# A new written order, other first loads and one slot array in a chunk attention and phase mixing kernel

## The chip, the cores and the metric

The kernel runs on one core of one Trainium2 chip. The metric is the time of one execution on the device in microseconds (us). One execution was also taken by the hardware profiler; all rows come from that trace. Engines: PE is TensorE (PEld its weight loads), DVE is VectorE, ACT is ScalarE, POOL is GpSimd, SP is SyncE, which only issues transfers here. The loads that POOL issues here change the type on the way (fp32 to fp16); the transfers of SP and ACT change no type.

## What is computed

There are 8 batches of 8 heads, 576 positions and 64 columns. First comes attention inside chunks of 64 positions, then a mixing layer over the 512 = 8 x 64 columns:

```
scores = q_c @ k_c^T / 8;  attn = softmax(scores);  x = attn @ v_c
theta = x @ w_theta
y = w_tok_r @ (x * cos(theta)) + w_tok_i @ (x * sin(theta))      # over positions
u = x + y
out = u + max(u @ w_ch, 0)
```

## The kernel before, in words

Batches go in four pairs, numbered 0 to 3. The 1152 positions of a pair are nine tiles of 128 rows: 0 to 3 of the first batch, 4 to 7 of the second, and 8 (MID), which holds the last 64 positions of both. Attention works on groups: A (tiles 0, 1), B (2, 3), C (4, 5), D (6, 7), M (8).

All work is written by hand as a list of steps, `ORDER`; each step calls one function, and each engine and each queue runs its own part of the list strictly in that order. A step is kind.place.slot: `S.0A.0` is the scores of pair 0, group A, into PSUM bank 0; `Y.12.7` is the mixing of pair 1, tile 2, in bank 7. For copies the last number is a buffer slot. The kinds:

- `qk` (load_qk, L161, issued at L168 and L173) and `v` (load_v, L180, issued at L192): loads by POOL, cast to fp16 on the way. `lt`, `ct` (L202, L205): w_theta in fp32 by SP, and its cast, half on ACT (L208), half on DVE (L210). `lc` (L212): w_ch by POOL. `lw` (L197): 128 rows of the token weights by POOL, in two transfers (L200).
- `Tq`, `Tk`, `T` (L248): DVE's 32 x 32 transposes of q and k (L257). `S` (L264): scores on PE (L272). `E` (L282): exp on ACT (L286). `V0`, `V1` (L293): products with v for heads 0 to 3 and 4 to 7 on PE (L306); v has a column of ones, so that they also give the row sums. `N0`, `N1` (L315): DVE's reciprocal (L321) and product (L323).
- `X` (L332): transposes of x on PE (L338), then `xa` or `xv`, a copy from PSUM on ACT (L358) or DVE (L356); or, in the place of both, `xd`, a transposing transfer by SP (L350).
- `H` (L364): x @ w_theta on PE (L370). `G` (L379): cos and sin on ACT (L384, L388); exp and sin lie in different tables, and a table load stands in front of an activation that needs the other one. `Z` (L392): zr = x cos, zi = x sin on DVE (L398 to L405).
- `TW`, `twv`, `twa` (L217, L232): PE's transposes of the token weights (L227) and their copies (L237 on DVE, L239 on ACT).
- `Y` (L431): nine matmuls of 512 columns a tile (L420); `Ya` and `Yb` are its first four and last five. `A` (L439): u = x + y on DVE (L441). `U` with `ua` or `uv` (L443, L449), or `ud` by SP (L454): the transpose of u. `W` (L462): u @ w_ch on PE (L466). `R` (L471): relu and sum on DVE (L473). `st`, `sa` (L479): the store on SP's or ACT's queue (L484, L487).
- `pre` (L136): fills of zeros, the column of ones, a first exp. `init` (L152): the identity, by POOL. `dm.n` (L155): n matmuls of zeros (L157).

Buffers come from a pool with one tag for each name and slot: eight for q and k, others for T, eT, xT, cos, sin, uT and o. The order begins and ends so:

```
pre.00 lt.00 ct.00 qk.0A.0 Tq.0A.0 Tk.0A dm.16.7 S.0A.0 v.0A E.0A.0 dm.4.7 V1.0A.2
init.00 V0.0A.4 ct.01 N0.0A N1.0A dm.8.7 X.0A.6 xa.0A.0 qk.0M.1 Tq.0M.1 Tk.0M dm.4.7
H.0A.0 S.0M.7 qk.0B.2 Tq.0B.2 E.0M.1 v.0M dm.11.7 V0.0M.4 Tk.0B v.0B lw.01 V1.0M.5
S.0B.2 N1.0M N0.0M dm.2.7 X.0M.6 E.0B.2 V1.0B.4 xa.0M.1 N1.0B V0.0B.2 N0.0B H.0M.7
G.0A.0 TW.01.4 twv.01 lw.03 X.0B.6 TW.03.2 lw.02 dm.1.5 TW.02.4 xv.0B.2 Z.0A twv.03
G.0M.1 Z.0M twa.02 H.0B.0 lw.00 Ya.02.6 G.0B.2 Z.0B qk.0C.3 Tq.0C.0 Tk.0C Ya.01.7
...
W.30.4 sa.27 R.36.2 sa.31 R.34.1 ud.38.0 ud.37.3 st.26 W.38.5 W.37.6 R.30.0 R.38.3 sa.30
st.36 R.37.5 sa.37 st.34 st.38
```

Of the kernel before, what the change touches and what calls it, by code (L numbers as in the profile page):

```python
# [38 lines left out]
Z.1D E.2A.1 V0.2M.7 R.10.3 V0.2A.3 V1.2A.0 V1.2M.5 N1.2A xa.2B.2 N0.2A W.07.2 Y.15.6
U.13.0 ua.13.1 N0.2M X.2A.1 qk.2C.5 xv.2A.3 R.07.2 H.2B.3 G.2B.1 N1.2M Z.2B T.2C.0  # L40
W.13.7 X.2M.0 xa.2M.0 H.2A.1 qk.2D.6 R.13.4 T.2D.2 v.3C H.2M.5 v.2D W.11.3 R.11.1 st.06
G.2A.2 qk.3A.7 Y.14.0 st.10 G.2M.0 sa.11 Z.2A A.15 ud.15.5 S.2D.1 S.2C.3 Z.2M Y.16.7
A.16 ud.16.6 E.2D.2 V1.2D.5 V0.2D.1 A.14 ud.14.4 N1.2D N0.2D E.2C.0 st.05 v.2C Y.18.3
V1.2C.4 N1.2C V0.2C.6 W.12.0 qk.3D.0 Y.21.1 A.18 qk.3B.1 A.21 N0.2C Y.23.4 Y.22.5
xd.2D.1 sa.07 st.13 T.3A.1 R.12.0 Y.17.6 xd.2C.2 H.2C.2 A.17 T.3B.2 H.2D.6 qk.3C.2 A.22
T.3C.0 A.23 Y.20.0 G.2C.1 v.3B S.3C.1 S.3A.3 U.18.5 A.20 Z.2C v.3A G.2D.2 W.14.6 st.12
Z.2D qk.3M.3 W.16.7 U.17.0 T.3D.0 v.3M R.16.3 ua.18.0 Y.24.5 E.3C.1 A.24 W.18.1 R.18.5
R.14.1 Y.26.2 T.3M.1 ud.20.2 S.3B.5 ua.17.1 S.3M.7 S.3D.0 st.16 A.26 E.3A.3 V0.3A.3
N0.3A E.3B.2 V1.3A.5 E.3M.0 W.15.2 N1.3A R.15.2 Y.25.7 ud.21.0 A.25 V1.3B.3 V0.3B.5
E.3D.3 V0.3M.0 v.3D N0.3M V1.3M.1 sa.14 W.17.2 N0.3B xd.3A.3 sa.18 N1.3B Y.27.7 W.21.0  # L50
# [14 lines left out]
def kernel(  # L65
# [23 lines left out]
    VP = D + 2  # L89
    scale = 1.0 / math.sqrt(D)  # L90
    half = [slice(0, CH), slice(CH, P)]
    quarter = [slice(32 * i, 32 * i + 32) for i in range(4)]

# [14 lines left out]
    bufs = ctx.enter_context(tc.tile_pool(name="bufs", bufs=1))  # L108
# [10 lines left out]
    wnat = const.tile([P, KT + 1, 2, S], FP16, name="wnat")  # L119
    v16 = const.tile([P, 2 * NT, H, VP], FP16, name="v16")  # L120
    wraw = const.tile([P, NDB, DM], FP32, name="wraw")
# [5 lines left out]
    def buffer(shape, name, slot, dtype=FP16):  # L127
        return bufs.tile(shape, dtype, name=name, tag=f"{name}{slot}")
# [6 lines left out]

    def setup(p, g):  # L136
        nc.vector.memset(zeros, 0.0)
        nc.vector.memset(pihalf, math.pi / 2.0)  # L138

        one = tmp.tile([P, 2, 32, 2], FP16, name="one")  # L140
# [6 lines left out]
        nc.vector.tensor_copy(  # L147
            out=v16[:, :, :, D], in_=one[:, 1, 0:H, 0].unsqueeze(1).broadcast_to((P, 2 * NT, H))
        )
        nc.scalar.activation(out=first, in_=pihalf, func=AF.Exp)  # L150
# [10 lines left out]
    def load_qk(p, g, slot):  # L161
        j0, bb, s0 = GROUPS[g]
        t = buffer([P, 2, H, 2, D], "qk", slot)
        st["qk", p, g] = t
        for w, ap in enumerate((q, k)):
# [6 lines left out]
            else:  # L172
# [5 lines left out]
                )  # L178

# [17 lines left out]
    def load_tok(p, tb):  # L197
        rows = min(P, S - tb * P)
        for ri, ap in enumerate((moe_w_tok_r, moe_w_tok_i)):
            nc.gpsimd.dma_start(wnat[0:rows, tb, ri], ap[tb * P : tb * P + rows, :])  # L200

    def load_theta(p, g):  # L202
        nc.sync.dma_start(wraw, moe_w_theta.rearrange("(a p) e -> p a e", p=P))

    def cast_theta(p, a):  # L205
        h = slice(2 * a, 2 * a + 2)
        if a == 0:
            nc.scalar.copy(out=wtheta16[:, h], in_=wraw[:, h])  # L208
        else:
            nc.vector.tensor_copy(out=wtheta16[:, h], in_=wraw[:, h])  # L210
# [6 lines left out]
    def tok_w(p, tb, b):  # L217
        m = min(P, S - tb * P)
        rows = slice(0, m)
        ps = banks(b, 2, FP16)[:, 0 : NT * m].rearrange("p (k t) -> p k t", k=NT)  # L220
        for kt in range(NT):
# [4 lines left out]
            for to, ri, s0, n in parts:  # L226
                nc.tensor.transpose(  # L227
                    ps[to, kt, :], wnat[rows, tb, ri, s0 : s0 + n], id16[rows, rows]
                )
# [311 lines left out]
```

## Time and profile before

| what | value |
|---|---|
| three runs | 202.27, 202.6 (median), 204.76 us |
| span of the profiled execution | 202.3 us |
| mean granted clock of TensorE | 0.986 |
| busy: PE, DVE, ACT, POOL | 183.1, 134.0, 90.5, 85.8 us |
| read from and written to HBM | 33.06 MB, 9.44 MB |
| POOL's queue: bytes written to the chip | 16.01 MB |

The profile gives no time of the whole execution beside the span, from the first to the last instruction; it lies 0.3 us under the median of the runs. A row of the timeline has its start, its length, the engine and line, the operation with out<-in, its count and, in brackets, how long the engine had stood idle and what ended that. A row of groups has busy time, mean ns of one, and idle time before. A row of windows has for each engine the busy time and, in brackets, the count of instructions, then the granted clock, the share of the transfer engines and GB/s. "Issue" is idle time for which the profile shows no release. Matmuls overlap in the records, so that busy PE time is not work.

### The profile page before, as it was taken

Reading aid. Unit: us, or ns where it says so; the run is one execution under the profiler, and the core shown is the slowest. Engines: PE = TensorE matmul, PEld = TensorE weight load, DVE = VectorE, ACT = ScalarE, POOL = GpSimd, SP = SyncE. Lnnn points to the kernel's source line nnn. Section 1 sums busy time; section 2 is a strip of 40 time slices with the busy share of each in tenths; the row PEclk is TensorE's granted clock in tenths of the full one; section 3 lists DMA queues with packets and bytes.
Section 4 is the critical chain, followed back from the end, with each engine's and each line's share of the span. In section 5 each row is a group of like instructions: output and inputs, shape, how many; then the busy total and the mean of one; then the engine's idle time right before and its main releaser. Section 6 shows DMA issues by size and latency. Waiting matters only on the chain.

```text
span 202.3 us, 5964 instructions
## 1 busy us (share of the span) xinstructions
PE 183.1 (90%) x2600; PEld 91.6 (45%) x2600; DVE 134.0 (66%) x240; ACT 90.5 (45%) x97; POOL 85.8 (42%) x121
## 2 busy tenths in 40 slices
PE   7369899999999998699899999799999999999980
PEld 2134554564546534354554444354644444444320
DVE  3137078888569777576867976657787965563560
ACT  2222199557993477059749700098404370400000
POOL 7587994795985867279564730000000000000000
PEclk9979999999999999999999999999999999999997
DMA  5999999999999999999999999605197865442776
GB/s 196 170 106 172 166 166 173 158 172 165 116 168 164 177 155 211 174 195 167 197 232 177 212 132 123 196 0 81 32 203 159 164 126 155 131 141 77 240 203 200
DMA packets 104602, 32.13 MB, mean 159 GB/s; under 512 B 97792, under 2 KB 99456, under 8 KB 104576
## 3 DMA queue, kind: packets, MB, share of 16 engines
q0 software_dynamic: 77232, 16.01, 99.9%
q1 hardware_dynamic: 24576, 10.75, 26.3%
q10 hardware_dynamic: 2768, 4.98, 7.1%
q8 instruction: 20, 0.33, 0.7%
q14 instruction: 6, 0.05, 0.2%
HBM read 33.06 MB, written 9.44 MB: 210 GB/s over the span
## 4 chain that ended last, share of the span: by engine, by line
PE 67%; DMA 12%; ACT 6%; DVE 5%; issue 4%; SPq 3%; POOL 0%; ACTq 0%; DVEq 0%; POOLq 0%
PE psum L420 25%; PE psum L466 13%; PE psum L370 13%; DMA uT<-x 5%; PE psum L272 5%; DMA qk<-in_k_dram 4%; PE psum L157 3%; PE psum L306 3%; DMA xT<-x 2%; PE psum L338 2%; SPq L350 2%; ACT eT L286 2%; ACT sin L388 2%; DVE T L257 2%; PE psum L227 1%
## 5 line engine op out<-in xcount | busy, mean ns | idle before, releaser
L192 POOL DMA_DIRECT2D v<-in_v_dram x56 | 41.7, 763 | 16.1 <-DMA qk<-in_k_dram 6.8
L420 PEld LDWEIGHTS <-wT 128*128 128x128 f16 (+1 forms) x360 | 30.8, 100 | 37.1 <-issue 3.0
L420 PE MATMUL psum<-zr,wT 128*128 128x512 f16 (+1 forms) x180 | 44.5, 381 | 0.0
L420 PE MATMUL psum<-zi,wT 128*128 128x512 f16 (+1 forms) x180 | 42.0, 379 | 1.6 <-issue 1.6
L441 DVE TENSOR_TENSOR x<-psum,x 128x512 f16<-128x512 f32 x36 | 24.5, 682 | 19.4 <-PE psum L420 18.1
L466 PE MATMUL psum<-wch,uT 128*128 128x512 f16 x144 | 35.4, 380 | 0.6 <-DMA uT<-x 0.3
L370 PE MATMUL psum<-wtheta,xT 128*128 128x512 f16 x144 | 33.8, 380 | 1.6 <-DMA xT<-x 1.0
L257 DVE STREAM_TRANSPOSE T<-qk 128x1024 f32<-128x1024 f32 (+3 forms) x25 | 25.0, 1013 | 7.6 <-DMA qk<-in_q_dram 6.8
L473 DVE SCALAR_TENSOR_TENSOR o<-psum,x 128x512 f32<-128x512 f32 x36 | 24.1, 681 | 6.8 <-PE psum L466 6.3
L384 ACT ACTIVATE cos<-psum,pihalf 128x1024 f16<-128x1024 f32 (+1 forms) x20 | 20.6, 1031 | 13.8 <-PE psum L370 13.4
L286 ACT ACTIVATE eT<-psum 128x1024 f16<-128x1024 f32 (+1 forms) x20 | 18.4, 939 | 18.6 <-PE psum L272 18.0
L323 DVE TENSOR_TENSOR x<-psum,recip 128x512 f16<-128x512 f32 (+1 forms) x40 | 25.5, 638 | 1.4
L384 ACT ACT_TABLE_LOAD x8 | 10.3, 1283 | 26.1 <-PE psum L370 20.1
L370 PEld LDWEIGHTS <-xT 128*128 128x128 f16 x144 | 13.3, 98 | 18.5 <-ACT xT L358 2.1
L466 PEld LDWEIGHTS <-uT 128*128 128x128 f16 x144 | 13.0, 98 | 15.5 <-DMA uT<-x 1.9
L272 PE MATMUL psum<-T 32*64 32x64 f16 x1152 | 13.9, 193 | 5.9 <-DVE T L257 5.0
L388 ACT ACTIVATE sin<-psum 128x1024 f16<-128x1024 f32 (+1 forms) x20 | 18.7, 937 | 0.0
L321 DVE RECIPROCAL recip<-psum 128x8 f32<-128x8 f32 (+1 forms) x40 | 7.8, 194 | 14.5 <-PE psum L306 14.1
L398 DVE TENSOR_TENSOR zr<-x,cos 128x1024 f16<-128x1024 f16 x16 | 11.0, 685 | 9.5 <-ACT cos L384 9.5
L173 POOL DMA_DIRECT2D qk<-in_q_dram x16 | 14.7, 917 | 5.4 <-DVE zi L399 2.3
L272 PEld LDWEIGHTS <-T 32*64 32x64 f16 x1152 | 11.9, 106 | 10.1 <-DVE T L257 6.0
L157 PE MATMUL psum<-zeros 128*128 128x512 f16 x46 | 14.6, 470 | 1.9 <-DVE pihalf L138 1.2
(43 smaller groups left out, 130.5 us busy)
## 6 DMA issues: line engine op xcount, KB each, us to landing
out_dram<-o ACTq DMA_DIRECT2D x17, 256.0 KB, 2.9
qk<-in_q_dram POOLq DMA_DIRECT2D x16, 256.0 KB, 7.5
qk<-in_k_dram POOLq DMA_DIRECT2D x16, 256.0 KB, 8.4
out_dram<-o SPq DMA_DIRECT2D x15, 256.0 KB, 3.9
v<-in_v_dram POOLq DMA_DIRECT2D x40, 64.0 KB, 7.3
v<-in_v_dram POOLq DMA_DIRECT2D x16, 128.0 KB, 8.2
wraw<-in_moe_w_theta_dram SPq DMA_DIRECT2D x1, 1024.0 KB, 5.5
wnat<-in_moe_w_tok_r_dram POOLq DMA_DIRECT2D x4, 144.0 KB, 5.0
```

Source lines behind the costliest of these rows:

```text
L192: nc.gpsimd.dma_start(v16[rows, slot + t, :, 0:D], v[b, :, t0 : t0 + m, :].rearrange("h s d -> s h d"),)
L257: nc.vector.transpose(to.bitcast(FP32).rearrange("p (x l s) -> p x s l", l=32, s=2), src.bitcast(FP32).rearrange("p (x s d) -> p x s d", s ...
L272: nc.tensor.matmul(ps[half[r ^ cc], r, h], t[quarter[c], 1, h, :, e], t[quarter[c], 0, h, :, e], start=(e == 0), stop=(e == 1), tile_posit ...
L286: nc.scalar.activation(out=eT[:, 0:n].rearrange("p r h i -> p (r h i)"), in_=st.pop(("ps_s", p, g)).rearrange("p r h i -> p (r h i)"), fun ...
L323: nc.vector.tensor_tensor(out=x.rearrange("p r (h d) -> p r h d", h=H // 2), in0=ps[:, :, :, 0:D], in1=recip[:, 0:n].broadcast_to((P, n, H ...
L370: nc.tensor.matmul(ps[:, j * DM : j * DM + DM], xT[:, j, a, :], wtheta16[:, a, :], start=(a == 0), stop=(a == NDB - 1),)
L384: nc.scalar.activation(out=cos[:, 0:n].rearrange("p j e -> p (j e)"), in_=ps, func=AF.Sin, bias=pihalf, scale=1.0,)
L388: nc.scalar.activation(out=sin[:, 0:n].rearrange("p j e -> p (j e)"), in_=ps, func=AF.Sin)
L420: nc.tensor.matmul(ps[half[b]] if j == MID else ps, w, z, start=(kt == 0), stop=(kt == 2 * KT),)
L441: nc.vector.tensor_tensor(out=x, in0=st.pop(("ps_y", p, j)), in1=x, op=ALU.add)
L466: nc.tensor.matmul(ps, uT[:, a, :], wch16[:, a, :], start=(a == 0), stop=(a == NDB - 1))
L473: nc.vector.scalar_tensor_tensor(out=o, in0=st.pop(("ps_w", p, j)), scalar=0.0, in1=st["x", p][:, j], op0=ALU.max, op1=ALU.add,)
```

## The change

- *First loads.* Group A of pair 0 comes by SP in fp32, in two halves of four heads (`qk0`, `qk1`: four transfers of 256 KB), and is cast in halves: `cx0` (q on DVE, k on ACT), `cv1` (both on DVE). Its T, S, E are made in halves too (`T0`, `S0`, `E0` and `T1`, `S1`, `E1`). POOL makes the identity and then loads groups M and B and the v of all three.
- *w_theta* comes by POOL, cast on the way (`lp`), behind those v.
- *Zeros* for the dummies are filled behind DVE's first cast; the column of ones (`on`) behind T1. There are 27 dummies instead of 46.
- *Tables.* Ahead of each E and G that needs the other table stands a one-element activation of that kind, which carries the table load and waits for no TensorE result.
- *One slot array.* q, k, T, token weights and the cos and sin of two-tile groups share 2048-column slots; eT, xT, o and the one-tile cos and sin share 1024-column slots; uT has 512-column slots. A step takes the slot that its last number names, and waits for the last reader of what was there.
- *Phase step by tile.* For 0A and 0B, `H0`, `G0`, `Z0` and `H1`, `G1`, `Z1` work on one tile each. `Ya` and `Yb` have four matmuls each, and `Ym` the ninth.
- *The last tile* in halves of 256 columns: `W0`, `R0`, `st0` and `W1`, `R1`, `sa1`. Four stores go by POOL (`sg`).
- *A new order.* U is made by TensorE for six tiles instead of nine.

The diff, cut to its core:

```diff
+NSLOTS = {"big": 19, "mid": 14, "uT": 10}
 ORDER = """
+init.00 qk0.0A.0 cx0.0A.1 qk1.0A.2 pre.00 dm.2.0 dm.4.1 qk.0M.3 dm.2.0 dm.12.1 Tq.0M.4 Tk.0M
+T0.0A.0 qk.0B.5 Tq.0B.3 Tk.0B S0.0A.2 S.0B.0 E0.0A.0 cv1.0A T1.0A E.0B.1 S.0M.2 v.0A v.0B dm.2.3
+v.0M S1.0A.4 on.00 V0.0A.6 lp.00 dm.1.0 N0.0A lw.01.1 V0.0B.0 N0.0B V1.0B.6 dm.4.3 E.0M.2
+V1.0M.0 N1.0B lw.00.0 E1.0A V1.0A.1 X.0B.3 lw.02.4 N1.0A N1.0M X.0A.6 xa.0B.3 H1.0B.1 G1.0B.0
+xv.0A.1 H1.0A.6 TW.01.2 G1.0A.4 H0.0A.0 V0.0M.1 N0.0M lw.03.2 H0.0B.7 twv.01 G0.0A.1 X.0M.6
+Z1.0A xa.0M.3 Z0.0A G0.0B.2 Z0.0B TW.00.4 twv.00 TW.02.2 twv.02 TW.03.0 twa.03 Ya.01.7 Z1.0B
+H.0M.6 G.0M.2 Ya.00.2 Ya.02.3 Yb.02 qk.0C.3 Tq.0C.2 Z.0M Ym.02 v.0C Tk.0C Yb.00 Ym.00 A.00
...
+N0.0C Yb.03 Ym.03 S.0D.0 A.01 U.01.7 N1.0C X.0C.4 qk.1A.4 T.1A.1 v.0D xv.0C.0 ua.01.1 v.1A
+S.1A.2 A.03 E.0D.2 V0.0D.4 N0.0D V1.0D.0 qk.1M.3 N1.0D H.0C.6 X.0D.4 lw.04.4 xv.0D.2 E.1A.3
+G.0C.1 V1.1A.0 V0.1A.2 H.0D.4 TW.04.6 N1.1A G.0D.2 Z.0C Ya.05.0 twa.04 N0.1A Ya.04.2 X.1A.3
+Ya.06.4 Z.0D Yb.06 Ym.06 qk.1B.0 T.1B.4 A.06 Yb.04 U.03.6 Yb.05 T.1M.0 Ym.05 A.05 Ym.04 ua.03.2
+U.02.6 S.1B.4 E.1B.2 v.1B A.04 qk.2B.1 Y.08.0 lc.00 xv.1A.3 ua.02.3 V1.1B.6 V0.1B.4 T.2B.4
+S.2B.2 N1.1B W.03.1 S.1M.6 E.1M.0 v.1M N0.1B X.1B.4 A.08 W.00.5 E.2B.2 U.04.6 uv.04.2 V0.1M.0
...
+E.2D.6 ud.17.3 R.13.8 qk.3M.4 X.2A.4 T.3M.3 S.3A.5 E.3A.10 Y.18.1 A.18 V0.2C.5 X.2M.2 N0.2C
+ud.15.0 W.07.3 v.2D R.07.1 xa.2A.11 H.2A.0 st.13 xv.2M.8 R.10.12 V0.2D.2 N0.2D V1.2D.4 Y.16.7
+G.2A.4 qk.3B.5 N1.2D H.2M.0 G.2M.6 xd.2C.13 xd.2D.11 T.3B.2 H.2C.1 A.16 ud.11.2 W.15.0 Z.2M
+H.2D.6 ud.12.5 st.04 G.2C.5 W.11.1 Z.2B V1.3A.2 Z.2A ud.14.0 qk.3D.0 Y.22.4 Z.2C ud.18.4 G.2D.6
...
+R.27.5 ud.35.5 sg.26 sg.22 W.38.3 Y.34.1 A.34 A.31 R.38.1 sa.03 Y.32.7 W.30.0 ud.31.4 Y.37.3
+R.30.10 A.37 W.36.0 A.32 R.36.4 st.30 ud.34.3 ud.37.7 W.21.1 R.21.10 W.31.7 ud.32.0 sa.38 sa.36
+sa.21 R.31.1 W.20.0 R.20.3 W.33.1 W.34.7 sg.27 st.31 st.20 R.33.5 sa.33 W.35.0 R.34.4 sa.34
+R.35.10 st.35 W.32.1 R.32.1 W0.37.7 R0.37.5 st0.37 W1.37.0 R1.37 sa.32 sg.25 sa1.37
 """.split()
...
+    arrays = {
+        name: const.tile([P, NSLOTS[name] * w], FP16, name=name)
+        for name, w in (("big", 2048), ("mid", 1024), ("uT", 512))
+    }
...
+    def table(func):
+        if st.get("table") != func:
+            nc.scalar.activation(out=first, in_=pihalf, func=func)
+            st["table"] = func
...
+    def load_qk_half(f):
+        def load(p, g, slot):
+            j0, bb, s0 = GROUPS[g]
+            t = big(slot, 1, FP32).rearrange("p (w h s d) -> p w h s d", w=2, h=HH, s=2)
+            st["stage", f] = t
+            for w, ap in enumerate((q, k)):
+                nc.sync.dma_start(
+                    t[:, w].rearrange("p h s d -> p h (s d)"),
+                    ap[2 * p + bb, f * HH : f * HH + HH, s0 : s0 + GT, :].rearrange(
+                        "h (p s) d -> p h (s d)", s=2
+                    ),
+                )
...
+    def cast_qk_half(f, engines):
...
+            for w, e in enumerate(engines):
+                copy = nc.scalar.copy if e == "a" else nc.vector.tensor_copy
+                copy(out=to[:, w], in_=t[:, w])
...
+    def load_theta_cast(p, g):
+        nc.gpsimd.dma_start(wtheta16, moe_w_theta.rearrange("(a p) e -> p a e", p=P))
...
+    def theta_tile(j):
+        def step(p, g, b):
+            ps = banks(b)
+            theta_mms(ps, st["xT", p, g][:, j])
+            st["ps_t", p, g, j] = ps
...
     KTS = {
-        "": range(2 * KT + 1),
-        "a": [0, 1, KT, KT + 1],
-        "b": [2, 3, KT + 2, KT + 3, 2 * KT],
+        "a": [0, KT, 1, KT + 1],
+        "b": [2, KT + 2, 3, KT + 3],
+        "m": [2 * KT],
     }
+    KTS[""] = KTS["a"] + KTS["b"] + KTS["m"]
...
+    def w_half(f):
+        def step(p, j, b):
+            ps = banks(b)[:, 0 : DM // 2]
+            channel_mms(ps, st["uT", p, j], columns[f])
+            st["ps_w", p, j, f] = ps
```

More of the change, by code (lines that the diff above doesn't have):

```diff
@@ L89 @@
     VP = D + 2
+    HH = H // 2
     scale = 1.0 / math.sqrt(D)
@@ L291, in exps, with exps_half, step @@
         )
+    def exps_half(f):
+        def step(p, g, slot=None):
+            if f == 0:
+                st["eT", p, g] = mid(slot).rearrange("p (r h i) -> p r h i", r=2, h=H)
+            table(AF.Exp)
+            nc.scalar.activation(
+                out=st["eT", p, g][:, :, f * HH : f * HH + HH],
+                in_=st.pop(("ps_s", p, g, f)),
+                func=AF.Exp,
+                scale=scale,
+            )
+        return step
     def attn(f):
@@ L360, in x_copy, with theta_mms @@
         return copy
+    def theta_mms(ps, xT):
+        for a in range(NDB):
+            nc.tensor.matmul(
+                ps, xT[:, a, :], wtheta16[:, a, :], start=(a == 0), stop=(a == NDB - 1)
+            )
     def theta(p, g, b):
```

289 lines of the change are left out of this document (172 added, 117 removed).

## The prediction

> **What bounds the kernel now.** I read the page first, then the chain of waits, the windows, and the timeline of the start, the stalls and the end.
>
> ```profile
> span 202.3 us, 5964 instructions
> ...
> PE 183.1 (90%) x2600; PEld 91.6 (45%) x2600; DVE 134.0 (66%) x240; ACT 90.5 (45%) x97; POOL 85.8 (42%) x121
> ...
> PE 67%; DMA 12%; ACT 6%; DVE 5%; issue 4%; SPq 3%; POOL 0%; ACTq 0%; DVEq 0%; POOLq 0%
> ```
>
> TensorE carries the chain. But busy time counts overlapping records and 46 dummies, so I price its real work from undisturbed pieces of the chain (start, us, what):
>
> ```profile
> 28.19 0.62 PE psum L227 x10
> ...
> 37.19 0.64 PE psum L272 x64
> ...
> 46.33 0.45 PE psum L306 x32
> ...
> 51.41 0.45 PE psum L338 x8
> ...
> 172.70 3.88 PE psum L420 x18
> ```
>
> A 512-column matmul takes 3.88/18 = 0.2156 us, a token transpose step TW 0.6, a score group S 0.64, both halves of V 0.45, a transpose 0.056. With 36 Y tiles of nine (69.8), 288 matmuls of H and W (62.1), 20 S (12.8), V (8.8), 92 X and 36 U transposes (5.2, 2.0) and TW (3.0), the real work is 163.7 us. The other 202.3 - 163.7 = 38.6 us are lost. Where?
>
> ```profile
> 10.00:20.00 10.00, 8.09 (x127) 3.84 (x128) 5.85 (x11) 2.04 (x2) 8.00 (x13) 0.83 1.62 138
> ...
> 190.00:203.00 13.00, 6.53 (x28) 2.30 (x26) 4.54 (x7) 0.00 (x0) 0.00 (x0) 0.89 0.71 217
> ```
> ```profile
> 1.19 5.75 PE L157 MATMUL psum<-zeros 128*128 128x512 f16 x16 [1.19 <-DVE pihalf L138]
> ...
> 6.28 1.04 ACT L208 CAST wtheta<-wraw 128x1024 f16<-128x1024 f32 x1 [4.05 <-DMA wraw<-in_moe_w_theta_dram]
> ...
> 9.39 0.71 DVE L257 STREAM_TRANSPOSE T<-qk 128x512 f32<-128x512 f32 x1 [6.85 <-DMA qk<-in_q_dram]
> 9.65 0.58 POOL L168 DMA_DIRECT2D qk<-in_k_dram  x1 [2.01 <-DMA qk<-in_q_dram]
> 10.90 0.71 DVE L257 STREAM_TRANSPOSE T<-qk 128x512 f32<-128x512 f32 x1 [0.80 <-DMA qk<-in_k_dram]
> ...
> 11.54 1.02 DVE L210 CAST wtheta<-wraw 128x1024 f16<-128x1024 f32 x1
> 11.67 0.71 PE L272 MATMUL psum<-T 32*64 32x64 f16 x64 [4.73 <-DVE T L257]
> ...
> 21.80 0.56 POOL L200 DMA_DIRECT2D wnat<-in_moe_w_tok_i_dram  x1
> ...
> 32.63 0.59 PE L420 MATMUL psum<-zr,wT 128*128 128x512 f16 x2
> ```
>
> Until the first Y at 32.6 TensorE has done S and V of three groups (1.9 + 1.3), X (1.1), 20 matmuls of H (4.3) and three TW (1.9), 10.5 us: 22.1 are lost there. At the end 28 matmuls (6.0 us) fill 190.0 to 196.9, 0.9 lost, and 5.4 follow: 6.3. The middle loses 38.6 - 22.1 - 6.3 = 10.2. Its visible waits:
>
> ```profile
> 75.66 0.70 PE L272 MATMUL psum<-T 32*64 32x64 f16 x64 [0.50 <-ACT sin L388]
> 76.73 0.69 PE L272 MATMUL psum<-T 32*64 32x64 f16 x62 [0.36 <-ACT sin L388]
> ...
> 82.91 1.04 PE L420 MATMUL psum<-zi,wT 128*128 128x512 f16 x4 [1.64 <-issue]
> ...
> 129.25 3.63 PE L370 MATMUL psum<-wtheta,xT 128*128 128x512 f16 x16 [1.01 <-DMA xT<-x]
> ```
> ```profile
> 0.00:82.50 82.50, 72.39 (x1247) 37.63 (x1247) 53.91 (x101) 46.07 (x49) 61.66 (x89) 0.98 1.70 165
> 0.00:99.70 99.70, 88.61 (x1503) 46.40 (x1503) 65.67 (x122) 57.25 (x61) 73.68 (x104) 0.98 1.75 167
> 0.00:116.50 116.50, 104.46 (x1759) 54.66 (x1759) 79.44 (x147) 68.09 (x73) 84.16 (x119) 0.99 1.76 173
> ...
> q8 instruction: 20, 0.33, 0.7%
> ...
> PE psum L306 <- issue: 1.9, 3, 0.9
> ```
>
> The windows end at three stalls put down to "issue" (with a fourth 1.64 + 1.9 = 3.5 us). Matmuls done by then: 1247, 1503, 1759, steps of 256, each with a weight load; and 0.33 MB in 20 fetches is 16 KB a fetch, about 5200/20 = 256 TensorE instructions. So I read these as waits for the next block of instructions, after blocks of small S and V matmuls.
>
> **The change, part by part.** *Start.* First q, k come as four 256 KB fp32 loads on SP. What SP moved in the first 15 us (40 slices of 0.375 us):
>
> ```profile
> GB/s 0 0 0 0 0 158 82 289 333 388 388 415 393 310 190 181 171 154 172 182 177 167 155 147 155 153 167 174 173 116 125 29 10 11 52 61 72 159 182 180
> ```
> ```profile
> L257 DVE STREAM_TRANSPOSE T<-qk 128x512 f32<-128x512 f32 x8 | 5.3, 686 | 7.6 <-DMA qk<-in_q_dram 6.8 <-DMA qk<-in_k_dram 0.8
> L323 DVE TENSOR_TENSOR x<-psum,recip 128x512 f16<-128x512 f32 x32 | 22.1, 692 | 1.1
> L384 ACT ACT_TABLE_LOAD x8 | 10.3, 1283 | 26.1 <-PE psum L370 20.1 <-DVE x L323 4.8 <-issue 1.1
> L384 ACT ACTIVATE cos<-psum,pihalf 128x512 f16<-128x512 f32 x4 | 2.8, 688 | 2.6 <-PE psum L370 2.6
> L388 ACT ACTIVATE sin<-psum 128x512 f16<-128x512 f32 x4 | 2.4, 602 | 0.0
> L147 DVE COPY v<-one 128x144 f16<-128x144 f16 x1 | 0.9, 882 | 0.0
> ```
>
> Theta's 1 MB moved from 1.9 to 5.5 and released ACT at 6.28; quarters of it give 4.0, 4.6, 5.3, 6.0 for the four loads. DVE casts at 4.0 (half of 1.02), then fills zeros: the 20 dummies, now behind that cast, run from 4.9 to 11.5 (16 took 5.75; later ones 0.22). POOL makes the identity (0.6), then loads 0M (256 KB in four pieces) and 0B. POOL's loads drain in order: the first 256 KB were there at 9.39, the second at 10.90, so 0B's k, the third, at about 12.4. Tq, Tk of 0M and T0.0A end near 11.3: scores of 0A at 11.5, as before. The gain comes after it. DVE works in order: Tk.0B to 13.2, two casts and T1.0A to 14.9, the ones column (0.88 + 0.4) to 16.2, four norms of 0.85 and one of 0.5 to 20.1, xv to 20.7. TensorE then runs four H tiles and TW.01 (4.1 us), 20.8 to 24.9. ACT needs four half pairs of cos and sin (0.69 + 0.60, 1.2 in pipeline) and a copy from 21.7: 27.1. Ya.01 takes bank 7, which G0.0B reads: 27.2. The second path, loads: theta's 0.5 MB replaces 0A's q, k on POOL's queue, so the last token weights, issued at 21.80 and landing 5 us later, still come near 26.8; TW.03 waits for them, in front of Ya.01. Both say 27.2. Work done by then 10.2, lost 17.0: **-5.1**. If SP's 512-byte rows run at half theta's rate, -2.5; if the first POOL loads land 2 us sooner, -7.
>
> By the Trainium skill (SBUF — State Buffer, SBUF: two separate sides) an fp32 copy on VectorE can lock GpSimd out while it writes descriptors, so that the three casts added here would cost up to 1.5 us and the sum be 198.4. The row nearest is the 1.02 us cast at 11.54 above, beside POOL's k load.
>
> *Transposes:* 12 fewer U on TensorE, 0.056 each: **-0.7**; their DMA replacements have 16 us and more of matmul work ahead of the W that reads them. *Tables:* the load (1.28) went behind the wait for TensorE; now a dummy activation takes it ahead. What showed on TensorE is 0.50 + 0.36: **-0.9** (0 to -1.3). *Phase step by tile:* two half operations for one, inside the chain above. *Instruction blocks:* as many instructions, and four blocks of under 3.7 us of matmul work beside the loads as before: **0** (-3.5 to +2).
>
> *Slots:* POOL's loads now wait for slots of the shared array, with those behind them. The tightest is lw.04, whose slot T.1A frees; from there to TW.04 TensorE has S.1A, V.0D, H.0C, X.0D, V.1A, H.0D, 5.45 us.
>
> ```profile
> DMA to landing us min/median/max: 4.2/5.1/7.2
> ...
> DMA to landing us min/median/max: 4.5/8.0/11.9
> ...
> 87.71 6.50 DMA uT<-x
> ...
> 190.49 3.45 DMA uT<-x
> ```
>
> Token loads (first row) give 0.55 + 5.1 - 5.45 = 0.2 late, at worst 2.2; S.1A itself waits for 1A, whose bytes come in the old sequence while TensorE is 5 us ahead: 0.8. Taken **+1.0** (0 to 3). *xd.2C, xd.2D:* from V0.2C to H.2C there are X.2M, W.07, H.2A, V.2D, Y.16, H.2M, 6.1 us; a norm and a transpose of 6.50 (the rate beside loads) need 7.5, 1.4 late, and 2D 1.6 more. Before lost 1.01 at this place. With 3.45, the rate without loads, nothing is late. Taken **+1.5** (-1 to 4), nearer the loaded row, since H.2C comes at about 109.
>
> *End:* the last ten W run without a wait, since A.37 and A.32 lie 6.9 us ahead of their W (-0.7); the last relu works on half a tile:
>
> ```profile
> 196.96 0.69 DVE L473 SCALAR_TENSOR_TENSOR o<-psum,x 128x512 f32<-128x512 f32 x1 [0.33 <-PE psum L466]
> ```
>
> Four stores go to POOL, which has no loads left then: 0. 0.69 becomes 0.4, its store of 128 KB lands 0 to 0.5 sooner. **-1.2** (-0.3 to -1.8).
>
> Sum: -5.1 - 0.7 - 0.9 + 1.0 + 1.5 - 1.2 = -5.4; 202.3 - 5.4 = **196.9**. The runs' median is 202.6, 0.3 above the profiled span.
>
> **Rivals.** (1) *The loads keep their pace.* The bytes on POOL's queue are the same, so what TensorE gains at the start it waits for later: start -4.0, slots +3, xd +4: 202.3 - 4.0 - 0.7 - 0.9 + 3 + 4 - 1.2 = 202.5, down to 199 with half of it. For it: the wait at 9.65, POOL standing until an earlier load has landed. Against: token and group loads before were ahead of use by some us. (2) *All goes well:* start -7, slots 0, xd 0: 192.5. (3) *The shared slots make it slower.* qk.2B waits for Z.0C, 9.8 us of matmul work ahead of S.2B; at the longest landing, 11.9, with 0.9 for the second issue and 1.2 for T.2B it is 4.2 late; qk.1A (11.9 ahead) 2.1, lw.04 2.2. 8.5 instead of 1.0: 204.4. It decides if the typical landing there is over 10; the median, 8.0, speaks against. (4) *The change does not bring the start forward:* the clock window 10 to 20 shows 0.83 after TensorE stood still for 4.73 us; if 0M lands over 3 us late, the clock halves again (up to 1.7) and Y starts near 30: 200. (5) *The issue waits are chance.* If they are not tied to blocks, the 3.5 us need not come back: 193.4. The Trainium skill (Runtime: NRT & Kernel Launch, Instruction fetch mechanics) speaks for that: crossing a 16 KiB boundary is mostly hidden, it says; the steps of 256 matmuls above speak against.
>
> **How the numbers follow.** Forecast (194 to 199) 0.55, (1) 0.17, (2) 0.12, (3) 0.07, (4) 0.06, (5) 0.03. The range 191 to 202.5 leaves out (3), and the tails. About 2% is what a measurement can tell from no change: under 198.5 lie (2), (5) and most of the forecast case, 0.66; over 206.7 only the worst of (3) and unseen cases, 0.05; between, 0.29.
>
> **What would show it.** In the changed profile: first Y near 27; scores of 0A near 11.5; no table load between TensorE's H and cos; a DMA wait at L460's matmuls near 109; "issue" waits at steps of 128 matmuls; the last relu of 256 columns. A first Y after 30, or waits on qk or token loads of over 3 us between 36 and 58, would make the prediction wrong.

## The result and the profile after

The changed kernel takes 207.33 us (median of 4 runs, 206.68 to 209.34), the kernel before 202.44: a ratio of 1.032, 95% interval 1.027 to 1.037. That is 3% slower, 4.9 us by the medians and 6.5 by the ratio, where 196.9 was forecast. Ratios below compare undisturbed runs only; a median is taken over all runs, and where both are given the ratio decides. A run lasts 1.7 to 2.3 us longer than the span of its core (207.65 against 205.6 here).

The page of the changed kernel, the lines that answer to those shown of before:

```profile
span 205.6 us, 5965 instructions
...
PE 183.8 (89%) x2573; PEld 91.1 (44%) x2573; DVE 136.9 (67%) x249; ACT 86.3 (42%) x108; POOL 87.0 (42%) x124
...
PEclk9985999999998899999999969999999999999999
...
PE 73%; DMA 14%; issue 3%; POOL 3%; DVE 3%; ACT 2%; DVEq 0%; POOLq 0%; ACTq 0%; SPq 0%
```

TensorE still carries the chain, with some 27 matmuls fewer, but DMA's share of the chain has grown from 12 to 14% and the clock has two dents behind the start. What TensorE waited for (us in total, times, longest):

```profile
PE psum L585 <- issue: 3.0, 1, 3.0
PE psum L336 <- DMA v<-in_v_dram: 1.9, 1, 1.9
PE psum L460 <- DMA mid<-x: 1.8, 2, 1.4
PE psum L400 <- DVE mid L450: 1.7, 1, 1.7
PE psum L585 <- DMA uT<-x: 1.2, 1, 1.2
PE psum L400 <- issue: 1.1, 1, 1.1
```

The chain of waits and two rows of TensorE say where (start, us, what):

```profile
60.92 2.97 issue
...
110.80 7.20 DMA out_dram<-mid
118.00 0.02 issue
118.02 0.42 DVE mid L450
...
163.19 4.14 DMA mid<-x
...
184.71 8.61 DMA uT<-x
```
```profile
165.11 1.90 PE L460 MATMUL psum<-wtheta,mid 128*128 128x512 f16 x8 [1.40 <-DMA mid<-x]
...
193.36 1.47 PE L585 MATMUL psum<-wch,uT 128*128 128x512 f16 x6 [1.18 <-DMA uT<-x]
```

And the windows show what a pause costs behind itself (the number after the engines is the granted clock):

```profile
15.00:20.00 5.00, 4.72 (x87) 2.09 (x85) 3.36 (x8) 1.13 (x3) 3.78 (x8) 0.50 1.28 165
...
60.00:65.00 5.00, 2.03 (x40) 1.36 (x33) 0.50 (x1) 3.90 (x5) 3.81 (x5) 1.00 2.48 146
65.00:70.00 5.00, 5.00 (x32) 1.99 (x30) 3.18 (x7) 0.00 (x0) 4.12 (x7) 0.66 1.73 176
115.00:120.00 5.00, 3.18 (x46) 1.58 (x45) 2.76 (x7) 2.11 (x3) 2.29 (x4) 1.00 2.27 179
120.00:125.00 5.00, 5.00 (x17) 1.77 (x16) 2.95 (x4) 1.16 (x2) 1.31 (x2) 0.66 2.12 129
```

So there are three new things. TensorE stands 2.97 us at a W at 60.9 without a releaser. At 110.8 a store is issued that lands after 7.2 us; a copy of a transposed tile into the same slot waits for it, and TensorE stands 1.7 us. Late DMA transposes stop H of 3C for 1.40 us until 165.1 and H of 3D for 0.37 until 167.4 (the piece at 163.19 is 3D's transfer), and W of tile 36 for 1.18 us until 193.4. By SP's order the transfer at 184.71 is `ud.36`, and W.36 is the first of the ten W that follow; the expectations of pe_turns and own_fix below call this wait that of tile 32. Behind the first two pauses the clock is 0.66 in a window of five microseconds, some 1.7 us lost each time. At the start the clock is at 0.50 from 15 to 20, and the first Y comes at 29.50:

```profile
13.25 1.29 PE L336 MATMUL psum<-big 32*64 32x64 f16 x96 [1.93 <-DMA v<-in_v_dram]
...
29.50 0.39 PE L540 MATMUL psum<-zr,wT 128*128 128x512 f16 x1
```

### The profile page after: what moved, and what is told of

The parts are those of the page before. It is cut to its first block, busy times and chain, and to the rows that moved or that the text cites. A ratio compares the mean times of both kernels' runs of the same rounds, so it can differ in the third digit from the quotient of the medians.

```text
span 205.6 us, 5965 instructions
## 1 busy us (share of the span) xinstructions
PE 183.8 (89%) x2573; PEld 91.1 (44%) x2573; DVE 136.9 (67%) x249; ACT 86.3 (42%) x108; POOL 87.0 (42%) x124
## 4 chain that ended last, share of the span: by engine, by line
PE 73%; DMA 14%; issue 3%; POOL 3%; DVE 3%; ACT 2%; DVEq 0%; POOLq 0%; ACTq 0%; SPq 0%
PE psum L540 32%; PE psum L460 15%; PE psum L585 11%; PE psum L336 5%; DMA out_dram<-mid 5%; DMA uT<-x 4%; PE psum L400 4%; DMA v<-in_v_dram 3%; PE psum L432 2%; DMA mid<-x 2%; PE psum L276 2%; PE psum L171 1%; DVE mid L590 1%; POOL big L182 1%; POOL big L187 1%
## 5 line engine op out<-in xcount | busy, mean ns | idle before, releaser
L540 PE MATMUL psum<-zr,wT 128*128 128x512 f16 (+1 forms) x180 | 62.4, 383 | 0.1
L540 PE MATMUL psum<-zi,wT 128*128 128x512 f16 (+1 forms) x180 | 59.7, 383 | 0.0
L585 PE MATMUL psum<-wch,uT 128*128 128x512 f16 (+1 forms) x148 | 35.6, 380 | 4.2 <-issue 3.0
L460 PE MATMUL psum<-wtheta,mid 128*128 128x512 f16 x144 | 35.1, 391 | 2.4 <-DMA mid<-x 1.8
L366 ACT ACTIVATE mid<-psum 128x1024 f16<-128x1024 f32 (+1 forms) x19 | 17.2, 933 | 34.3 <-PE psum L336 25.4
L590 DVE SCALAR_TENSOR_TENSOR mid<-psum,x 128x512 f32<-128x512 f32 (+1 forms) x37 | 24.4, 670 | 10.1 <-PE psum L585 7.1
L298 DVE STREAM_TRANSPOSE big<-big 128x1024 f32<-128x1024 f32 (+3 forms) x25 | 25.3, 1020 | 5.3 <-DMA big<-in_q_dram 3.3
L482 ACT ACTIVATE big<-psum,pihalf 128x1024 f16<-128x1024 f32 x14 | 15.6, 1114 | 23.5 <-PE psum L460 23.5
L460 PEld LDWEIGHTS <-mid 128*128 128x128 f16 x144 | 13.5, 101 | 20.2 <-DMA mid<-x 3.8
L336 PE MATMUL psum<-big 32*64 32x64 f16 x1152 | 14.5, 194 | 2.6 <-DMA v<-in_v_dram 1.9
## 6 DMA issues: line engine op xcount, KB each, us to landing
v<-in_v_dram POOLq DMA_DIRECT2D x16, 128.0 KB, 7.2
out_dram<-mid ACTq DMA_DIRECT2D x7, 128.0 KB, 2.6
```

Of the source, the lines that this page charges most:

```text
L298: nc.vector.transpose(out.bitcast(FP32).rearrange("p (x l s) -> p x s l", l=32, s=2), in_.bitcast(FP32).rearrange("p (x s d) -> p x s d", ...
L336: nc.tensor.matmul(ps[half[r ^ cc], r, h], t[quarter[c], 1, h, :, e], t[quarter[c], 0, h, :, e], start=(e == 0), stop=(e == 1), tile_posit ...
L366: nc.scalar.activation(out=eT[:, 0:n].rearrange("p r h i -> p (r h i)"), in_=st.pop(("ps_s", p, g)).rearrange("p r h i -> p (r h i)"), fun ...
L460: nc.tensor.matmul(ps, xT[:, a, :], wtheta16[:, a, :], start=(a == 0), stop=(a == NDB - 1))
L540: nc.tensor.matmul(ps[half[b]] if j == MID else ps, w, z, start=(kt == 0), stop=(kt == 2 * KT),)
L585: nc.tensor.matmul(ps, uT[:, a, :], wch16[:, a, cols], start=(a == 0), stop=(a == NDB - 1))
```

## The experiments

Three theories stood at the beginning. *Slots*: waits for slots of the shared arrays, directly or through the load queue, cost the time. *Blocks*: TensorE waits for its next 256 instructions wherever the last 256 took too little time, and the new order has denser places. *Order*: the new order brings transposes too late, whatever the slots. An edit of slots changes numbers in ORDER and the sizes of the arrays only, so no work and no order.

### Slots alone, one array at a time

```diff
-NSLOTS = {"big": 19, "mid": 14, "uT": 10}        # own_mid
+NSLOTS = {"big": 9, "mid": 30, "uT": 10}
-... R.13.8 ... st.13 xv.2M.8 ... xd.2C.13
+... R.13.10 ... st.13 xv.2M.15 ... xd.2C.18

-... qk.1A.4 T.1A.1 ... lw.04.4 ... qk.2B.1       # own_big
+... qk.1A.16 T.1A.17 ... lw.04.3 ... qk.2B.5
```

own_mid, expected:

> The changed kernel with 30 slots instead of 14 in the array that exponentials, transposed tiles and outputs share, given out in turn, so that no copy meets an output that is still being stored. In the changed kernel a transposed copy of 2M stood 2.2 us for a store's landing (7.2 us), TensorE stood 1.75 us behind it at 116.7, and the granted clock was 0.66 from 120 to 125. Slot theory: that wait and the slow clock behind it go, 1.7 + 1.8 us: 203.8. Rival (the new order brings 2M's transposed copy late anyway, or another wait takes the place): 206.5 to 208.

Measured: 207.15 us, ratio 1.027 (1.015 to 1.038). The rival held. The wait for the store is gone, and 2.5 us later the next one stands in its place (the chain, then TensorE's row):

```profile
114.50 8.23 DMA mid<-x
122.73 0.05 issue
122.78 3.48 PE psum L460 x8
```
```profile
122.78 1.46 PE L460 MATMUL psum<-wtheta,mid 128*128 128x512 f16 x3 [3.46 <-DMA mid<-x]
```

The DMA transpose of 2C took 8.23 us beside loads and stores. In the changed kernel that wait was largely hidden under the store's wait and the slow clock.

own_big, expected:

> The changed kernel with its 19 large slots given out in turn (it uses 9 of them), so that POOL's loads of q, k and token weights need not wait for DVE's transposes. Slot theory: POOL's waits for DVE (8.5 us) go, loads run ahead, DMA no longer stands still at 40 to 45 and 80 to 85; but TensorE waited for such a load nowhere by over 0.5 us, so at most 1 us is gained: 206 to 207.5. Rival (loads that run further ahead keep the queue full, so that transposes by DMA and instruction fetches land later): 208 to 210.

Measured: ratio 1.018 (1.003 to 1.033), runs from 204.8 to 212.0. That is some 2.8 us less than the changed kernel, but the intervals overlap, so the time alone doesn't show a gain. What the trace shows lies not where I looked. The DMA engines' busy tenths of own_mid and of own_big, 40 slices of 5.1 us:

```profile
DMA  5999999999999999999999999304498596139996
```
```profile
DMA  5999999999999999999999936305398796149995
```

With free slots POOL ran ahead, the last load had landed at 117.1 instead of 127.5 (125.5 in the changed kernel), and H of 2C, at 121, waited for nothing: its transpose, issued at 117.2, took 3.1 us. So slots of loads cost time neither where the load waits nor where its data are used, but where a DMA transpose is issued while loads still run.

### The blocks moved

```diff
+            if kind == "ds":
+                for _ in range(int(at)):
+                    nc.tensor.matmul(psum[0:CH, ...], zeros[0:32, 0:CH], zeros[0:32, 0:CH], tile_position=(0, 0))
-... T0.0A.0 qk.0B.5 Tq.0B.3 Tk.0B S0.0A.2 S.0B.0
+... T0.0A.0 qk.0B.5 Tq.0B.3 Tk.0B S0.0A.2 ds.32.7 S.0B.0     # shift32; ds.64.7 in shift64
-pre.00 lt.00 ct.00 ... dm.16.7 S.0A.0
+pre.00 lt.00 ct.00 ... dm.16.7 ds.56.7 S.0A.0               # before_shift, on the kernel before
```

> The changed kernel with 32 tiny matmuls (64 TensorE instructions with their weight loads, some 0.4 us) put where TensorE waits for 0B's k. Outputs and work are as before. Block theory (TensorE waits for its next 256 instructions where the last 256 took under some 5 to 6 us of work while loads run): the waits at instructions 1984 (2.97 us, at 60.9) and 2752 (1.13 us, at 87.8) move to what were instructions 1920 and 2688: the block before the first took 4.3 us, so it waits 0.6 to 1.8; before the second 2.0 us, so it waits 2.9 to 4, in the scores near 84.9. Rival (the waits belong to that W and that V): they stay where they are with 3.0 and 1.1 us. Time 206 to 210 by the first, 207.3 by the second.

> The same with 64 tiny matmuls (128 instructions). Block theory: waits at what were instructions 1856 (block of 3.2 us: a wait of 1.7 to 2.9 in the scores near 58.4) and none over 1 us at 2624 (5.3 us) and 3648 (5.1 us): 205.5 to 207. Rival: the waits stay at that W and that V: 207.3.

> The kernel before with 56 tiny matmuls (112 TensorE instructions) put where TensorE waits 5 us for the first scores; nothing else changed. Block theory: the edges of the blocks of 256 move by 112 instructions, away from the dense places: the waits at 2496, 3008 and 3520 (2.0, 0.8, 1.0 us) go, the densest blocks then take 4.2 to 4.9 us, so 0.5 to 1 us is left: 199 to 200. Rival (the waits belong to places or to chance): 202, with waits of the same sum.

Measured: shift32 207.69 us (203.5 to 209.6), shift64 210.85, ratio 1.043 (1.032 to 1.055), before_shift 1.011 (1.002 to 1.021). The gains did not come (shift32's runs are too scattered for a ratio), but the places are those of the theory. Matmuls done where TensorE stood, in the changed kernel (two rows), shift64, before_shift (two) and own_fix (two, below):

```profile
0.00:60.80 60.80, 52.24 (x986) 28.75 (x987) 41.52 (x82) 29.91 (x42) 45.47 (x69) 0.94 1.55 159
0.00:87.70 87.70, 76.17 (x1370) 40.51 (x1370) 60.70 (x117) 44.29 (x59) 61.48 (x90) 0.94 1.55 148
```
```profile
0.00:61.60 61.60, 53.33 (x987) 29.93 (x987) 39.60 (x79) 29.52 (x41) 44.52 (x67) 0.94 1.46 151
```
```profile
0.00:44.50 44.50, 41.13 (x735) 22.41 (x735) 25.91 (x53) 21.21 (x25) 35.86 (x55) 0.96 1.64 176
0.00:144.50 144.50, 135.33 (x2271) 71.60 (x2271) 98.75 (x176) 78.94 (x85) 85.69 (x121) 0.98 1.55 159
```
```profile
0.00:16.60 16.60, 10.78 (x223) 5.23 (x224) 7.58 (x18) 4.61 (x7) 13.69 (x25) 1.00 1.51 160
0.00:110.10 110.10, 98.58 (x1757) 52.48 (x1758) 78.39 (x147) 60.02 (x78) 81.14 (x115) 0.97 1.72 159
```

Together with 1247, 1503 and 1759 of before they lie on one ladder with steps of 128 matmuls, that is 256 instructions with the weight loads: 223, 735, 986 to 987, 1247, 1370, 1503, 1757 to 1759, 2271. (A few semaphore instructions count too and make the differences of up to six.) In shift64, 64 more matmuls were done ahead, so the wait came 64 matmuls earlier in the work, in scores instead of W; before_shift left its old places and stood in two new ones. The other profiles agree: all 56 waits of TensorE of 0.3 us and more for "issue", in seventeen profiles, lie on this ladder.

The traces also hold what these waits are for. They record each fetch of 16 KB of instructions (queue q8). The one at 61.47 ended at 62.42, and TensorE went on at 63.89; the one at 86.48 ended at 87.45, and TensorE went on at 88.92. All 56 waits end in this way, 1.2 to 1.8 us behind the end of such a fetch, so the cause is seen directly and not only by counting.

Two sizes were wrong. In shift32 I expected 0.6 to 1.8 us at the first place and 2.15 came; at the second I expected 2.9 to 4 and none is seen. And a block needs time without loads too: the chain of before_shift has, at 144, when the loads were over,

```profile
143.09 1.23 PE psum L267 x87
144.32 0.14 PE psum L301
144.46 1.48 issue
145.95 0.45 PE psum L301 x31
```

Its block took 1.8 us of work, and 3.3 us lie between its first instruction and the next block's; beside the loads these are 6.1 us for the wait at 60.9 (57.8 to 63.9). The fetch itself took about 1 us in both places, but it began 0.9 us behind the first instruction of the block at 142.7 and 3.7 us behind that at 57.8. I had priced only the dense places under the loads, so moving the edges exchanged known waits for others.

### The old order in the new code

```diff
 # after.py with the steps of before's ORDER, the last tile in halves; slots:
-... qk.1A.5 T.1A.2 ... lw.04 ... qk.2B.0 qk.3A.7              # before, a pool for each kind
+... qk.1A.8 T.1A.10 ... lw.04.2 ... qk.2B.7 qk.3A.7            # old_order: 10 large slots, in turn
+... qk.1A.5 T.1A.10 ... lw.04.18 ... qk.2B.0 qk.3A.7           # old_slots: 8 + 3 + 3 + 5, as before
```

> The order of before in the code of the changed kernel: early table loads, one slot array per width with slots given out in turn, and the last tile in halves; start, loads, stores and the middle stay in the old order. Theory (what is lost lies in the new order): tables 0.9 and end 1.2 us are gained as forecast, 202.4 - 2.1 = 200.3. Rival (the shared arrays or the early table loads cost time by themselves): 203 or more.

> The kernel old_order with other slot numbers only: in the shared arrays every kind of data has as many slots of its own as in before (8 for loads of q and k, 3 for their transposes, 3 for cos and sin, 5 for token weights), where old_order gave 10 large slots out in turn. In old_order POOL stood 7.8 and 5.2 us for slots, the last load landed at 134.9 instead of some 125, and TensorE stood 4.9 us for the DMA transposes behind it. Slot theory: those waits go, the loads end near 125, the wait before H of 2D is 1 to 1.5 again: 200 to 202, with the tables' and the end's gain. Rival (the array, the early tables or the end cost the time): 207 to 210, with the same waits.

Measured: old_order 210.25 us, ratio 1.034 (1.023 to 1.044); old_slots 202.26 us, ratio 0.999 (0.996 to 1.003). Between these two only slot numbers, the sizes of the arrays and the array of the one-tile cos and sin differ, and by the ratios that is worth 7 us. The profiled executions took 212.13 and 208.07 us. POOL's waits in old_order, and what followed on the chain:

```profile
POOL big L186 <- DVE x L418: 7.8, 1, 7.8
POOL big L186 <- DVE big L299: 5.2, 1, 5.2
```
```profile
125.68 8.75 DMA mid<-x
134.43 0.05 issue
134.48 1.89 PE psum L461 x4
```

POOL stood 13 us for slots, the last load landed at 134.9, the transpose of 2C, issued at 125.7, took 8.75 us beside the loads and TensorE stood 4.6 us. In old_slots the last load landed at 126.6 and TensorE stood nowhere for 2C or 2D. So the shared array costs nothing by itself; too few load slots do. And the early table loads and the split last tile, together forecast at -2.1, brought -0.1 with an interval of about 0.8 us to either side. The two waits of scores for ACT at 75.7 and 76.7 are gone as forecast, but the next block's edge, which comes right behind, does not come sooner for that: the wait there was 4.2 us in the profiled execution of old_slots and 1.6 in before's. As that execution was 5.8 us above its kernel's median, this doesn't show where the forecast gain went.

### The new start with the old rest

```diff
 # after.py: the new ORDER up to Z.0M, then before's steps without those done
-... Z0.0B TW.00.4 ... Z1.0B ... Ya.01.7 H.0M.6 ...
+... Z0.0B TW.00.4 ... Z1.0B H.0M.5 G.0M Z.0M Ya.02.6 qk.0C Tq.0C Tk.0C Ya.01.7 Ya.03.2 ...
 # start_slots: start_only with slots as in old_slots; start_fill_end: and dm.8.7 behind S0.0A, last tile in halves
 # start_shift: start_slots with ds.84.7 at the start for 4 of its dummies; best: and X/xa for xd of 2C, 2D, last tile in halves
-... pre.00 dm.2.0 dm.4.1 ... dm.12.1
+... pre.00 ds.84.7 dm.2.0 dm.4.1 ... dm.8.1
```

> The new order up to the phase step of 0M, then the rest in the order of before, in the code of the changed kernel with slots given out in turn; the end as before. Theory (the start's gain is real, the new order's middle gives it back): first Y 3 us earlier than in before, at 29.5, and tables 0.9: 202.4 - 3.9 = 198.5. Rival (the loads keep their pace, so TensorE waits later for what it gained): 201 to 203, with waits for q, k or token loads after 40 us.

> The kernel start_only with slots in the shared arrays as many for each kind as in before. POOL waits less for slots, so the loads end no later than in before. Theory (the new start is worth 1.1 us at the first Y, 29.6 against 30.75 in the kernels with the old start): 201.3, 1.1 below before. Rival (the loads keep their pace, TensorE waits later for what it gained): 202.4.

> start_slots with 8 dummies (1.7 us) where TensorE waits for 0B's k, and with the last tile in halves. Theory (the filled gap keeps the clock, which brought the first Y from 29.5 to 28.4 in fill_start; the halves bring 0.3 to 1): 1 to 2 us below start_slots. Rival (what the first Y gains is lost at the instruction waits behind it, and the end is bound by the stores): as start_slots within 0.5.

> The kernel start_only with the slots as many for each kind as in before, and with 84 tiny matmuls in place of 4 dummies at the start (160 TensorE instructions more), so that the edges of the blocks of 256 fall between the dense places. Block theory: the waits that start_only shows at its instructions 448, 2496 and 3008 (1.1, 1.9, 3.0 us) shrink to 1 to 2 in all: span 198.5 - 4 = 194 to 195, time 197 to 198. Rival (the waits come elsewhere, or the start is later by the tiny matmuls): 201 to 202.

> start_shift with 2C and 2D turned by TensorE and ScalarE instead of by DMA (0.9 us more TensorE work) and the last tile in halves. Theory (the DMA transposes behind the loads cost 1 to 2 us there when the loads end late; the halves bring 0.3 to 1): 0.3 to 1.5 us below start_shift. Rival (nothing waits there any more once the loads are early, so only the added work and the end count): the same as start_shift within 0.5.

Measured ratios: start_only 0.997 (0.992 to 1.003), start_slots 1.001 (0.996 to 1.006), start_fill_end 1.003 (0.999 to 1.008), start_shift 1.018 (1.012 to 1.024), best 1.011 (1.005 to 1.017). None beats the kernel before: start_slots and start_fill_end came out as their rivals said, start_shift was slower than both of its theories said, and best lies 1.5 us below start_shift by the ratios, with intervals that overlap. The first Y was at 29.63 in start_only, and this explains half of the miss of its expectation: the three kernels with the old start that were profiled here (old_order, old_slots, before_shift) have it at 30.76 to 30.78, not at the 32.63 of the profiled execution of before.

```profile
30.76 0.59 PE L415 MATMUL psum<-zr,wT 128*128 128x512 f16 x2
```

The new start is worth 1.1 us there. What start_only was ahead, it stood still at two edges of blocks:

```profile
78.77 0.48 PE L399 MATMUL psum<-v,mid 64*64 64x65 f16 x36 [1.69 <-issue]
...
96.42 0.39 PE L399 MATMUL psum<-v,mid 64*64 64x65 f16 x18 [2.78 <-issue]
```

start_shift had no wait at these two places and none of over 0.6 us between 49 and 125, as the theory says, but it stood at the ladder's places before and behind (1.2 us until 41.4, 2.9 until 47.6, 1.6 until 145.2), for DMA transposes (2.0 us until 128.0, 2.1 until 196.7), and its tiny matmuls put the first Y at 31.4.

### The clock at the start

```diff
-... S0.0A.2 S.0B.0
+... S0.0A.2 dm.8.7 S.0B.0
```

> The changed kernel with 8 dummies more (1.7 us) where TensorE waits for 0B's k after the first scores. Clock theory (the clock fell to 0.50 in 15 to 20 because TensorE stood still before): the clock stays at 0.9 or more there, the later dummies take 0.22 instead of 0.47 us, and the first Y comes 1.3 us earlier, at 28.2: 206. Rival (DVE's norms or the loads set the first Y): it stays at 29.5 whatever the clock: 207.3.

Measured: 207.62 us, ratio 1.020 (1.008 to 1.033). The clock was 1.00 in all three windows from 10 to 25, and the first Y came at 28.45, 1.05 us earlier. The time shows at most part of it. That the dummies did this is not shown: own_mid and own_big have the same start without them, and there the clock stayed at 1.00 from 15 to 25 behind waits for 0B's scores of 0.94 and 1.44 us instead of 1.93, with the first Y at 28.47 and 27.83. In own_fix and pe_turns, again the same start, the clock fell and the first Y came at 29.94 and 29.84. So the clock is worth some 1 to 2 us at this start, and whether it falls changed from execution to execution.

### The late transposes away

```diff
-... xd.2C.13 xd.2D.11 ... xd.3C.6 ... ud.32.0                                  # pe_turns, own slots in both arrays
+... X.2C.6 ... xa.2C.0 ... X.2D.3 ... xa.2D.0 ... X.3C.7 xa.3C.0 ... U.32.6 ua.32.0
-... xd.3C.6 ... ud.32.0                                                     # own_fix, own slots in both arrays
+... X.3C.7 xa.3C.0 ... U.32.6 ua.32.0
```

> The changed kernel with own slots in both arrays, and with 2C, 2D, 3C and tile 32 turned by TensorE and copied by ScalarE instead of turned by DMA (28 more TensorE transposes, 1.6 us). Theory (TensorE stands for DMA transposes that come late behind loads and stores: 3.8 us before H of 2C in the kernel with own slots, 1.1 to 2.4 before H of 3C, 1.0 to 1.6 before W of 32, and 1.8 for the slow clock behind the first): 207 - 8 + 1.6 = about 201. Rival (the loads or the instruction waits behind them take the place): 205 or more.

> The changed kernel with own slots in both arrays (17 large and 18 of half the size, given out in turn), and with 3C and tile 32 turned by TensorE and ScalarE instead of by DMA (0.7 us more TensorE work); 2C and 2D stay with DMA, since the loads then end by 117. Theory (slots and late DMA transposes cost the time): own_big, whose profiled span was 204.4, without its waits before H of 3C (2.4 + 0.7) and W of 32 (1.0): span 201, time 203. Rival (instruction waits of 2.5 to 3 us each, and the slow clock behind them, hold it whatever the slots): 205 to 207.

Measured: pe_turns 205.43 us, ratio 1.015 (1.004 to 1.027); own_fix 203.85 us, ratio 1.012 (1.007 to 1.017), against 1.032 of the changed kernel. Neither edit removes the late transpose of tile 36: both turn tile 32 on TensorE, which had waited for nothing. pe_turns gives out 12 large slots where own_fix has 17; POOL still stood 7.6 us for two of them and its last load landed at some 126.7. It also made a wait of its own: the copy of 2C stood on ACT ahead of cos and sin of 2A, and H of 2C waited 2.1 us for the PSUM bank that these read. own_fix leaves 2C and 2D to DMA behind loads that end earlier. What its TensorE waited for:

```profile
PE psum L400 <- issue: 3.7, 2, 2.0
PE psum L336 <- issue: 1.9, 1, 1.9
PE psum L585 <- issue: 1.0, 1, 1.0
...
PE psum L585 <- DMA uT<-x: 0.5, 1, 0.5
```

The waits for stores and transposes, 1.8 + 1.7 + 1.2 us in the changed kernel, are down to half a microsecond, and the ratio fell by 0.020, 4 us. The transpose of tile 36 took 6.9 us there instead of 8.6 and came in time; why it was faster is not shown. What remains is 6.6 us of waits at edges of blocks, in the kernel before 3.5 and in the changed kernel 4.1.

## Why the prediction was wrong

It failed in its sum of small terms, and in the base that it counted from. Neither of the two signs that were to show it wrong came (a first Y after 30, a wait of over 3 us for q, k or token loads): the time was lost where it named no sign. By its own steps:

- *The base.* I took the profiled execution (202.3) for one like the median run, "0.3 above the span". A run is some 2 us longer than its span, so that execution was one of some 204, if this held for it too, and it was late at the start: its first Y at 32.63 instead of 30.77. That alone is 2 us of the promised gain.
- *Start, -5.1.* 0A's scores came at 10.87 (11.5 forecast) and 0B's wait was as computed, but the first Y came at 29.5, not 27.2. Rival (4), named at 6%, happened in part: TensorE stood 1.93 us until 13.25, the clock halved, and dummies that should have taken 0.86 us took 1.9; with the clock kept, the same start has its first Y at 27.8 to 28.5. Against the usual old start the gain is 1.3 us in the changed kernel and 2.3 to 2.9 with the clock kept; no kernel with it beats the kernel before by more than can be measured.
- *Tables, -0.9,* and *end, -1.2.* The two waits for ACT are gone, and the tail behind the last matmul is 4.3 us instead of 5.4, though the last relu still waited for a store that held its slot:

```profile
202.07 0.76 DVE L590 SCALAR_TENSOR_TENSOR mid<-psum,x 128x256 f32<-128x256 f32 x2 [0.90 <-DMA out_dram<-mid]
```

  In old_slots the two together moved the time by nothing that can be measured.
- *Instruction blocks, 0 (-3.5 to +2).* The mechanism was right, and the runs with moved edges bear it out against rival (5), and against the Trainium skill (Runtime: NRT & Kernel Launch, Instruction fetch mechanics), by which crossing a 16 KiB boundary is mostly hidden: with 2.97 us at one of them the measurement decides. The size was not: 2.97 + 1.13 us, and the clock at 0.66 behind the first (some 1.7 us), in place of 3.5. I had counted the blocks of under 3.7 us of work and priced them as alike; the new order put one of 3.1 us ahead of the W at 60.9, and its fetch began 3.7 us late.
- *Slots, +1.0 (0 to 3).* The place was wrong. I priced loads against their first use, lw.04 above all, and no such use waited by over 0.5 us. The wait came where a slot's last reader is a store, which I had not priced (1.7 us and a slow clock), and through the load queue: loads that wait for slots end later, and DMA transposes issued before that end take 5.4 to 10.5 us instead of 3.1. own_big, old_order and old_slots show this way, rival (3)'s, but through another door.
- *xd.2C and xd.2D, +1.5 (-1 to 4).* Right in mechanism and within its range: 3.5 us in own_mid, none in own_big, hidden under the slot's wait in the changed kernel. H.2C came at 123, not 109, but the loads still ran and the transpose took 8.3 us, not 6.5. That the clock falls behind such a pause was not in the price.
- *Not priced at all:* xd.3C and xd.3D (1.4 + 0.4 us) and ud.36 (1.2 us), all without loads. I looked no further than 2D. The end term has the last ten W run without a wait, from A.37 and A.32; the first of the ten is W.36, and it waited. Its `ud.36` was issued at 184.7, when seven stores were in flight, and took 8.6 us, with 7.5 us of work to cover it.
- The rule weighed beside the start, the Trainium skill's (SBUF — State Buffer, SBUF: two separate sides) that an fp32 copy on VectorE can lock GpSimd out, isn't needed for any of this. No run here tells whether it took part.

Added up against the forecast's span of 196.9, the trace of the changed kernel gives: start 2.3 (29.5 for 27.2), blocks 2.3 (5.8 for 3.5), slots with 2C and 2D 0.9 (1.7 and the slow clock's 1.7 for 2.5), 3C and 3D 1.8, tile 36 1.2, in all 8.5 of the 8.7 us to 205.6. This is an estimate: waits that follow each other may hide each other.

In all, of the 6.5 us that the ratio gives some 4 go with own slots and the edits of own_fix (shown by own_fix as a whole, not by each edit). The rest, about 2.4 us above before, stands at edges of blocks in own_fix's trace; that it would go with sparser blocks was not shown, since every shift of the edges found new dense places.

What stays open: why the fetch for the same edge begins 2.2 us behind the block's first instruction in old_slots (a wait of 1.7 us), 4.1 in old_order (3.2) and 1.3 in start_only (none); and why shift32 did not wait at its second place.

## What to carry to other kernels

Ask of each buffer not only whether its data come in time, but what its last reader is (the store above held it for 7.2 us) and what a late load queue does to the transfers issued before its end. Price an order by the time that each run of 256 TensorE instructions takes, since a gain ahead of a dense one may be given back there. And before counting from a profiled execution, see how its start and its time stand to other runs of the same kernel: here 2 us of the "gain" were chance.

## What the runs showed of the hardware

- TensorE's next block of 256 instructions came 3.1 to 3.3 us after the first instruction of the block before when no loads ran (three kernels, at 140 to 146), and 3.7 to 8.7 beside loads; a block with less work than that shows the difference as "issue". In 56 of 56 such waits TensorE went on 1.2 to 1.8 us behind the end of a 16 KB fetch of instructions.
- In seventeen profiles 33 of 51 pauses of TensorE of 1.4 us and more behind the start were followed by a stretch at half clock, which began within the pause or at most 2 us behind it; the shortest with one lasted 1.48 us (before_shift), the longest without 3.21 (old_order, fill_start). The stretches last 3.4 us or 6.8, so that a window of 5 shows 0.66. With 8 dummies in the pause at the start (fill_start) the clock stayed at 1.00; so it did in own_mid and own_big without them.
- The DMA transpose of 2C, 256 KB, took 3.1 us after the loads' end (own_big) and 8.2 to 8.8 when issued before it (own_mid, the changed kernel, old_order); a 128 KB one took 8.6 among seven stores and 2.4 alone.
